# One attention-and-convolution kernel: fillers freed of the accumulator bank, a gate step in four operations, and more score sets in 29-row form

## The chip, the cores and the metric

The kernel runs on one core of a Trainium2 chip. The core has a matrix engine (PE, with its weight loads listed apart as PEld), a vector engine (DVE), a scalar engine (ACT), a general engine (POOL, which here mostly issues DMAs) and a queue engine (SP) that issues DMAs. Each engine works through its own instructions in the order in which they were written; semaphores hold an instruction until what it needs has been done. The metric is the time of one execution on the device in microseconds (us), the median over repeated runs.

## The reference

A row of the input gets an attention result `a` and a state-space convolution result `b`, mixed by a gate of one number for each row:

```python
S, D, H, Dh, N = 2048, 448, 16, 28, 256
q = (x @ wq).reshape(B, S, H, Dh).transpose(0, 2, 1, 3)
k, v = x @ wk, x @ wv                         # one key and one value head for all 16 query heads
scores = einsum("bhqd,bkd->bhqk", q, k) * Dh ** -0.5
a = (softmax(scores) @ v).transpose(0, 2, 1, 3).reshape(B, S, H * Dh) @ wo

dt = exp(log_dt)[:, None]
P = exp((dt * (A_re + 1j * A_im))[:, :, None] * arange(S))
K = einsum("dn,dnl,dn->dl", C, P, dt * Bc).real   # one kernel of 2048 taps for each channel
b = causal_convolution(x, K) + x * Dskip

g = sigmoid((x * gate_w).sum(-1, keepdims=True))
out = g * a + (1 - g) * b
```

All inputs and the output are bf16.

## The kernel before

**Attention.** The 2048 queries by 16 heads against 2048 keys are cut into 1024 score tiles of 128 keys by 512 columns. Sixteen groups of 64 tiles follow one another; a group is 512 queries by four heads, and its tiles run over 16 key tiles and the four heads (`h = t % 4`). The tiles are taken in 410 *sets*, by turns of three tiles (even sets) and two (odd sets). For each set:

- PE writes the scores into PSUM (`psS`, five banks in rotation). There are two forms. The *full form* (`full`, L1380) multiplies 128 rows of `kT` by a masked copy of the queries, `qM`, in which the rows of all other heads are zero; the two or three matmuls of a set run one after the other. The *29-row form* (`row`, L1357) takes the 29 rows of the tile's head alone, at rows 32h of the array, so that the matmuls of a set, having different heads, lie in different row strips and run side by side. `qM` is filled by a DMA from `qT`, so that the first tiles of a group have to use the 29-row form in any case (`NEWQ = 15`). The last 24 tiles are cut otherwise and have lines of their own (L1368).
- ACT takes the exp of the whole set into a ring of 15 tiles in SBUF (`expT`, L1412). Each exp needs its scores and free places in the ring.
- PE multiplies four exp tiles with the values (*PV*, L1433) and adds them up in the accumulator bank `psB` (key `("b", 6)`) over the 16 key tiles. At the end of a group DVE copies the bank out (`norm`, L1157), and the softmax's denominators, normalisation and output projection (L1137) follow.

**Convolution.** Beside this, DVE builds tables of powers for 32 channels at a time (`tables`, L972 to L1008, in 14 rounds), PE turns them into convolution kernels (`kgen`, L1031), and these are written to a scratch tensor in DRAM and read back as Toeplitz tiles `T` by SP's DMAs. PE convolves with them (`conv`, L1098, and L1119 for the transposed result), and DVE adds the result to the output tiles. `conv` number c first writes half c % 2 of the buffer `cst`; the other use of its second half is to hold the zeros that the fillers below read.

**The gate.** `prep_gate` transposes 1 - g by a matmul (L749), copies it, and spreads it with four small f32 matmuls (L760) in one operation. A copy of the result, `omq`, scales the convolutions. The two PE operations are placed behind sets 30 and 35 (`GATE`).

**Fillers.** Two kinds of matmul add zeros or write into unused banks, to keep PE busy. `warm` (L1333, 43 of them) is an operation of its own behind some of the first 64 sets; it adds zeros to the accumulator bank and declares that it writes that bank, so a PV that comes later in the program is ordered behind it, and it behind the PV before. `filler` (L1339) is put in by the planner where it finds a gap on PE.

**Order.** A planner written in Python, `Prog.schedule`, fixes the order of each engine before the program is written out. Each operation has an estimated length, a priority `pr` (small is early), its dependences by keys that it reads and writes, and an array mode (`mode`: "q" for 29-row, "c" for PV and convolution, "h" for `kgen`, "f" for full). It takes, over all engines, the operation that can start first; among those that can start at the same time the smallest `pr`. Score sets have 0, PV 0.5, `kgen` 1.15, `conv` 1.6, `warm` 1.95, the gate 2. `pg.after[a] = b` keeps a behind b in the plan. A dependence between two operations of PE orders them and needs no semaphore. `psb` marks the operations of the accumulator bank: 1 for a PV in the midst of a group, 2 for its last one; `opened` is true while a group is being added up. `act` is the share of its time that an operation counts in the planner's measure of how busy PE was, which must be under 0.8 over 4 us for a planner's filler.

Of the kernel before, what the change touches and what calls it, by code (L numbers as in the profile page):

```python
# [12 lines left out]
P = 128  # L13
# [32 lines left out]
XDVE = ((1, 0), (1, 1), (1, 2))  # L46
WARM = 64
HELD = ((27, 3), (27, 9), (27, 15), (27, 21))
ROWS = 400
NEWQ = 15  # L50
LASTQ = 13
STORES = (338, 341, 366)
# [43 lines left out]
class Prog:  # L96
# [15 lines left out]
    LAZY = {1.15: 200.0, 1.55: 200.0, 1.58: 200.0, 1.6: 200.0}  # L112
    LATE = 1000.0
    FILL, FWIN, FLOW = 215.0, 4000.0, 0.8

    def __init__(self, nc, es):
        self.nc, self.es = nc, es
# [70 lines left out]
    def schedule(self):  # L188
        ops = self.ops
# [11 lines left out]
        ready = {e: [] for e in ENG}  # L201
# [22 lines left out]
        while done < n:  # L224
            best = None
            for e in ENG:
                T = free[e]
                for i in ready[e]:
                    o = ops[i]
                    r = max(rt[i], T)  # L230
                    if o.lock is not None:
                        L = min((x for x in locks if x[0] is None), key=lambda x: x[1], default=None)
                        if L is None:
                            continue
                        r = max(r, L[1] + (300.0 if o.pr >= 2 else 0.0))
                    for k in o.comm or ():
                        if k in comm:
                            r = max(r, ops[comm[k]].end)
                    if e == "pe":
                        j = (npe + o.ni - self.FIRST - 1) // self.BLOCK + 1  # L240
                        if j < len(block):
                            r = max(r, block[j])
                            if o.pr >= 1 and block[-1] > r:
                                left = self.FIRST + (len(block) - 2) * self.BLOCK - npe - o.ni
                                r = max(r, block[-1] - left / self.NEED)
                    if o.slot is not None and o.slot[0] == "T" and self.spaced[0] < r < self.spaced[1]:
                        r = max(r, lastT + self.GAP)
                    key = (r, o.pr, i)
                    if best is None or key < best[0]:
                        best = (key, e, i)  # L250
# [25 lines left out]
                mode = o.mode  # L276
            if e == "pe":
                past.append((r, r + o.ns * o.act))
                opened = o.psb == 1 if o.psb else opened
            if e == "pool" and o.slot is None:  # L280
                for d in reversed(order[e]):
                    if ops[d].slot is None:
# [148 lines left out]
class Kernel:  # L431
# [311 lines left out]
    def prep_gate(self):  # L743
        pg = self.pg
        X = ("gx",)
        px = self.grp()
        ogT = Sub(self.acc, 512)
        self.gate = []
        o = pg.op("pe", lambda e: e.matmul(px.v(0, 16, 0, [[1, 128]]), self.gt.v(0, P, 16, [[1, 16]]),  # L749
                                       self.identg.v(0, P, 0, [[1, P]]), start=True, stop=True, tile_position=(0, 0),  # L750
                                       skip_group_check=True), 400,
              rd=["og", ("kst", 0)], wr=[X], pr=2, lock=px)
        self.gate.append(o.i)
        pg.op("dve", lambda e: e.tensor_copy(ogT.v(0, 16, 0, [[1, 128]]), px.v(0, 16, 0, [[1, 128]])), 200,
              rd=[X], wr=[("acc", 1)], pr=2)

        def mm(e):
            for mu in range(2):
                for par in range(2):
                    r = e.matmul(px.v(0, P, 64 * mu, [[1, 64]]), self.sel.v(0, 16, 128 * (1 + (1 - mu) - par), [[1, P]]),  # L760
                                 ogT.v(0, 16, 64 * par, [[1, 64]]), start=(par == 0), stop=(par == 1), tile_position=(0, 0),
                                 skip_group_check=True)
            return r
        o = pg.op("pe", mm, 800, rd=[("acc", 1)] + [("sel", k) for k in range(3)], wr=[X, "onw"], pr=2)
        self.gate.append(o.i)
        pg.op("dve", lambda e: e.tensor_copy(self.omq.v(0, P, 0, [[1, 128]]), px.v(0, P, 0, [[1, 128]])), 200,
              rd=[X], wr=["omq"], pr=2, unlock=px)
# [543 lines left out]
    def main(self):  # L1311
# [32 lines left out]
        def qk(s):  # L1344
            ts = sets[s]
            bs = [bank[t] for t in ts]
            bk = [("b", b) for b in bs]

            def row(e):
                if ts[0] >= NLAST:  # L1350
                    for x in range(2):
                        for t, b in zip(ts, bs):
                            r = part(e, t, b, x, True)
                    return r
                for t, b in zip(ts, bs):
                    i, kt, h = dec(t)
                    r = e.matmul(self.psS.v(0, P, 512 * b, [[1, 512]]),  # L1357
                                 kT.v(32 * h, DH + 1, 128 * kt, [[1, 128]]),
                                 qT.v(32 * h, DH + 1, 512 * (i % 2), [[1, 512]]),
                                 start=True, stop=True, tile_position=(32 * h, 0), skip_group_check=True)  # L1360
                return r

            def part(e, t, b, x, row):
                half, kt, h = declast(t)
                kt += x
                o = self.psS.v(0, P, 512 * b + 256 * x, [[1, 256]])
                if row:
                    return e.matmul(o, kT.v(32 * h, DH + 1, 128 * kt, [[1, 128]]),  # L1368
                                    qT.v(32 * h, DH + 1, 512 + 256 * half, [[1, 256]]),
                                    start=True, stop=True, tile_position=(32 * h, 0), skip_group_check=True)  # L1370
                return e.matmul(o, kT.v(0, P, 128 * kt, [[1, 128]]),
                                self.qM.v(0, P, XQ + 512 * h + 256 * half, [[1, 256]]),
                                start=True, stop=True, tile_position=(0, 0), skip_group_check=True)

            def full(e, t, b):
                if t >= NLAST:
                    part(e, t, b, 0, False)
                    return part(e, t, b, 1, False)
                i, kt, h = dec(t)
                return e.matmul(self.psS.v(0, P, 512 * b, [[1, 512]]), kT.v(0, P, 128 * kt, [[1, 128]]),  # L1380
                                self.qM.v(0, P, (i % 2) * XQ + 512 * h, [[1, 512]]),
                                start=True, stop=True, tile_position=(0, 0), skip_group_check=True)
            if s < 6 or s >= 14 and (len(ts) == 3 or ts[0] % 64 < NEWQ or s >= ROWS):
                rd = set()
                for t in ts:
                    i, kt, h = dec(t)
                    rd |= {("q", i % 2), ("kT", (kt if t < NLAST else declast(t)[1]) // 4)}
                o = pg.op("pe", row, 220, rd=sorted(rd, key=str), wr=bk, pr=0, mode="q", ni=2 * len(ts))
                o.act = 0.25 * len(ts)
            else:  # L1390
                for t, b in zip(ts, bs):
                    i, kt, h = dec(t)
                    kt = kt if t < NLAST else declast(t)[1]
                    o = pg.op("pe", lambda e, t=t, b=b: full(e, t, b), 220, rd=[("qM", i % 2), ("kT", kt // 4)],
                              wr=[("b", b)], pr=0, mode="f", ni=2)
            if s in GATE:
                pg.after[self.gate[GATE.index(s)]] = o.i
            if s < WARM and ts[0] % 64 < 52 and (ts[0] < 64 or ts[0] % 64 > 14):
                f = pg.op("pe", warm, 215, rd=[("cst", 1), "id"], wr=[("b", 6)], pr=1.95)
                pg.after[f.i] = o.i  # L1400
            if s == len(sets) - 2:
                pg.after[o.i] = self.prevset
            self.prevset = o.i
            if s in STORES:
                self.hold.append(o.i)
            es = [ring[t] for t in ts]
            ew = [("e", x) for x in es]
            for t in ts:
                x = ring[t] if t <= RING else 0
                ew += ["Wk"] if x == RING - 1 else ["Wv", "Wvg", "Wm"] if x == RING - 2 else self.xk(2) if 9 <= x < 13 else self.xk(3) if 5 <= x < 9 else []  # L1410
            n = len(ts)
            o = pg.op("act", lambda e: e.activation(expT.v(0, P, 512 * es[0], spread(es, n)),  # L1412
                                                self.psS.v(0, P, 512 * bs[0], spread(bs, n)),
                                                AF.Exp, scale=SQ), 46 + 428 * n, rd=bk, wr=ew, pr=0)
            self.lastexp = o.i
# [118 lines left out]
```

## Time and profile before

| | |
|---|---|
| median of 3 runs | 501.09 us (500.85 to 501.88) |
| the profiled execution | 500.49 us |
| its span in the profile | 498.7 us |
| first exp starts, last exp ends (L1412) | 21.71 us, 492.41 us |
| score matmuls in full form (L1380) | 316, each 383 ns |
| score matmuls in 29-row form (L1357) | 684, each 385 ns |
| fillers L1333, L1339 into the accumulator bank | 43 and 146 |
| DVE, last table instruction (L1008) | 447.94 us |

The span begins at the first instruction and ends with the last. A row of a group has the line of the kernel, the engine and operation, what is written and read, shapes, the count, and behind the bar the busy time in us, the mean of one in ns, and the idle time of the engine just ahead of them with what ended it. A row of the timeline has the start in us, the time that the merged instructions cover in us, engine, line, operation, and in brackets the idle time before it and what ended that. Times of matmuls overlap: a matmul of 512 columns is shown with some 0.38 us, while the next one in a run starts 0.22 us after it.

The granted clock of PE over some stretches (each line: the stretch, its length, busy us and instructions of each engine, the clock, the share of the DMA engines, GB/s):

```profile
26.00:34.00 8.00, 7.68 (x42) 2.26 (x40) 8.00 (x14) 7.76 (x7) 0.59 (x1) 1.00 0.38 46
76.00:100.00 24.00, 23.51 (x294) 9.05 (x295) 23.90 (x40) 24.00 (x22) 8.59 (x17) 1.00 0.80 230
447.00:480.00 33.00, 31.93 (x779) 17.74 (x777) 8.86 (x17) 31.98 (x29) 5.23 (x10) 1.00 0.80 238
```

The engines stand in the order PE, PEld, DVE, ACT, POOL.

### The profile page before, as it was taken

The page shows a single profiled execution, that of the slowest core. Times are in us where ns is not written, and L with a number is a line of the kernel's source. Part 1 is how long each engine was busy: PE and PEld are TensorE (multiplying, and loading weights), DVE is VectorE, ACT ScalarE, POOL GpSimd, SP SyncE. Part 2 cuts the span into 40 slices and gives each one's busy share as a digit, 9 for nine tenths or more (in the row PEclk, how much of TensorE's full clock was granted, in tenths as well). Part 3 has the DMA queues.
Part 4 walks back from the last instruction along what each step waited for, and adds up shares of the span by engine and source line. Part 5 has one row for each costly group of instructions (what it writes and reads, how often), then busy time and mean ns, then how long its engine had stood idle before and what let it go on. Part 6 is the DMA issues. An engine that isn't in the chain of part 4 may idle for free.

```text
span 498.7 us, 17357 instructions
## 1 busy us (share of the span) xinstructions
PE 478.2 (96%) x7643; PEld 217.7 (44%) x7643; DVE 456.0 (91%) x868; ACT 484.6 (97%) x436; POOL 197.5 (40%) x362
## 2 busy tenths in 40 slices
PE   8899999999999999999999999999999999999997
PEld 6432242453434435453452543545334354445543
DVE  6999999999999999999999999989999999992225
ACT  6999989999999999999999999999999999999995
POOL 8411034342242466276265456552733342521110
PEclk9999999999999999999999999999999999999999
DMA  8945008719248783945729595594690849657842
GB/s 252 268 57 113 1 16 229 213 34 315 77 118 265 204 217 87 308 108 165 242 36 268 155 288 138 141 220 112 171 265 19 231 129 340 213 164 215 257 131 70
DMA packets 91767, 85.44 MB, mean 171 GB/s; under 512 B 24970, under 2 KB 86716, under 8 KB 91692
## 3 DMA queue, kind: packets, MB, share of 16 engines
q1 hardware_dynamic: 80794, 72.49, 49.8%
q0 software_dynamic: 10624, 11.70, 10.5%
q8 instruction: 60, 0.98, 0.8%
q10 hardware_dynamic: 274, 0.14, 0.1%
q14 instruction: 15, 0.12, 0.1%
HBM read 76.36 MB, written 5.23 MB: 164 GB/s over the span
## 4 chain that ended last, share of the span: by engine, by line
ACT 77%; PE 15%; DMA 2%; SPq 0%; issue 0%
ACT expT L1412 77%; PE psS L1380 2%; PE psS L1357 2%; PE psB L1433 2%; DMA T<-KP_scratch 2%; PE psX L1098 1%; PE psS L1098 1%; PE psS L1031 1%; PE psB L1333 1%; PE psS L1368 1%; PE psS L1242 0%; PE psB L1427 0%; SPq L166 0%; PE psX L1031 0%; PE psX L1119 0%; PE psB L1339 0%
## 5 line engine op out<-in xcount | busy, mean ns | idle before, releaser
L1412 ACT ACTIVATE expT<-psS 128x1536 bf16<-128x1536 f32 (+1 forms) x410 | 464.8, 1363 | 3.5 <-PE psS L1357 1.4
L972 DVE TENSOR_TENSOR tab<-tab,mbf 128x512 bf16<-128x512 bf16 (+4 forms) x140 | 139.2, 996 | 0.0
L1357 PE MATMUL psS<-qT,kT 29*128 29x512 bf16 x684 | 95.7, 385 | 10.5 <-ACT expT L1412 6.4
L1433 PE MATMUL psB<-expT,vaug 128*32 128x512 bf16 x1000 | 99.7, 390 | 0.2 <-DVE acc L1157 0.2
L1380 PE MATMUL psS<-qM,kT 128*128 128x512 bf16 x316 | 95.1, 383 | 0.8
L166 POOL DMA_DIRECT2D KP_scratch<-kstg x104 | 58.1, 565 | 75.5 <-DVE kstg L1043 74.0
L987 DVE TENSOR_TENSOR tab<-tab 128x256 bf16<-128x256 bf16 (+4 forms) x140 | 77.0, 571 | 0.0
L1433 PEld LDWEIGHTS psB<-expT,vaug 128*32 128x32 bf16 x1000 | 25.6, 93 | 72.9 <-issue 69.9
L1357 PEld LDWEIGHTS psS<-qT,kT 29*128 29x128 bf16 x684 | 23.7, 91 | 62.9 <-ACT expT L1412 51.9
L166 POOL DMA_DIRECT2D U<-in_A_x_dram x60 | 39.9, 669 | 25.0 <-DMA U<-in_A_x_dram 10.3
L166 POOL DMA_DIRECT2D qM<-qT x64 | 32.5, 516 | 39.4 <-DVE qT L889 29.3
L1339 PE MATMUL psB<-ident,one 128*128 128x512 bf16 x146 | 47.2, 384 | 0.0
L1098 PEld LDWEIGHTS psS<-T,U 128*26 128x26 bf16 (+3 forms) x1792 | 35.7, 138 | 14.9 <-issue 10.2
L166 POOL DMA_DIRECT2D rdenB<-R_scratch x60 | 31.0, 523 | 28.0 <-DMA R_scratch<-denT 27.9
L1098 PE MATMUL psS<-T,U 128*26 128x128 bf16 (+3 forms) x1792 | 41.0, 226 | 1.1 <-DMA T<-KP_scratch 1.1
L1098 PE MATMUL psX<-T,U 128*26 128x128 bf16 (+3 forms) x1600 | 38.9, 227 | 0.7 <-issue 0.7
L1098 PEld LDWEIGHTS psX<-T,U 128*26 128x26 bf16 (+3 forms) x1600 | 32.6, 139 | 11.9 <-issue 9.5
L166 POOL DMA_DIRECT2D denT<-acc x15 | 10.8, 717 | 56.4 <-DVE acc L1157 47.7
L1001 DVE TENSOR_TENSOR tab<-tab,tmp 128x1984 bf16<-128x1984 bf16 x28 | 32.5, 1177 | 0.0
L1380 PEld LDWEIGHTS psS<-qM,kT 128*128 128x128 bf16 x316 | 19.5, 97 | 24.8 <-ACT expT L1412 15.3
L995 DVE TENSOR_TENSOR tmp<-tmp,mq 128x64 bf16<-128x64 bf16 (+4 forms) x70 | 25.3, 361 | 0.3
L918 DVE TENSOR_TENSOR msq<-T 128x512 f32<-128x512 f32 (+1 forms) x40 | 24.6, 616 | 0.0
(191 smaller groups left out, 511.9 us busy)
## 6 DMA issues: line engine op xcount, KB each, us to landing
T<-KP_scratch SPq DMA_DIRECT2D x212, 272.0 KB, 5.6
rdenB<-R_scratch POOLq DMA_DIRECT2D x60, 64.0 KB, 2.5
U<-KP_scratch SPq DMA_DIRECT2D x12, 272.0 KB, 4.9
U<-in_A_x_dram SPq DMA_DIRECT2D x20, 112.0 KB, 4.6
qM<-qT POOLq DMA_DIRECT2D x64, 32.0 KB, 3.9
tab<-in_A_x_dram SPq DMA_DIRECT2D x4, 448.0 KB, 5.2
KP_scratch<-kstg POOLq DMA_DIRECT2D x104, 16.0 KB, 1.7
xT<-XS_scratch POOLq DMA_DIRECT2D x3, 448.0 KB, 4.3
```

The lines of the kernel that those rows point to most:

```text
L166: return [e.dma_start(o, i, **kw) for o, i in pairs]
L918: pg.op("dve", lambda e: e.tensor_tensor(m2(msq), z2, z2, ALU.mult), el(2 * n), rd=[kr, ki] + first, wr=["msq"], pr=pr)
L972: mul = lambda e, o, a, b: e.tensor_tensor(o, a, b, ALU.mult)
L987: vo(lambda e, dv=dv, tv=tv, k=k: e.tensor_tensor(dv, dv, tv, ALU.add if k else ALU.subtract), n, [kt[k], kd[k]], [kd[k]], 1.92 if lv else ...
L995: vo(lambda e, w=w, lv=lv: e.tensor_tensor(rho.v(0, P, (32 - 2 * w) * 2, [[64, 32], [2, w], [1, 2]]), rho.v(0, P, (32 - w) * 2, [[64, 32], ...
L1001: vo(lambda e, k=k: e.tensor_tensor(tab.v(0, P, FM + k * FP + 2, [[64, 32], [2, 31], [1, 2]]), tab.v(0, P, lm + k * PL + 62, [[64, 32], [- ...
L1098: r = e.matmul(ps.v(32 * j, 32 - m0, 128 * k, [[1, 128]]), self.U.v(0, P, (4 * gi + j) % UA // UC * UW + (2 * m0 + par) * UC + (4 * gi + j ...
L1339: return e.matmul(t.v(0, P, off, [[1, 512]]), self.one.v(0, P, 2, [[0, P]]), self.ident.v(0, P, 0, [[0, 4], [1, P]]), start=b != 6, stop=b ...
L1357: r = e.matmul(self.psS.v(0, P, 512 * b, [[1, 512]]), kT.v(32 * h, DH + 1, 128 * kt, [[1, 128]]), qT.v(32 * h, DH + 1, 512 * (i % 2), [[1, ...
L1380: return e.matmul(self.psS.v(0, P, 512 * b, [[1, 512]]), kT.v(0, P, 128 * kt, [[1, 128]]), self.qM.v(0, P, (i % 2) * XQ + 512 * h, [[1, 51 ...
L1412: o = pg.op("act", lambda e: e.activation(expT.v(0, P, 512 * es[0], spread(es, n)), self.psS.v(0, P, 512 * bs[0], spread(bs, n)), AF.Exp, ...
L1433: r = e.matmul(self.psB.v(32 * h, 32, 0, [[1, 512]]), vaug.v(0, P, 32 * kt, [[1, 32]]), expT.v(0, P, 512 * ring[t], [[1, 512]]), start=(kt ...
```

## The change

Four things, in the order of the diff below.

`ROWS` goes from 400 to 320, and the condition on the form of a set is written anew: every three-tile set takes the 29-row form (before, sets 6, 8, 10 and 12 had the full form), and so do the two-tile sets from 320 on (before, from 400 on). 74 of the 316 matmuls in full form change.

`warm` no longer declares a write of the accumulator bank. It gets `psb = 3` instead: the planner places such an operation only while a group is open, and where an operation of priority 0 or less on PE is due to become ready in the first 175 ns of the filler (its 215 ns less `NEAR` = 40), it counts the filler as ready only behind that operation. A filler does not change `opened`.

The four small matmuls of the gate become four operations of 200 ns each in the plan, in place of one of 800 ns. The first is kept behind set 35; the others follow by their dependence.

```diff
-ROWS = 400
+ROWS = 320
...
     FILL, FWIN, FLOW = 215.0, 4000.0, 0.8
+    NEAR = 40.0
...
+                    if o.psb == 3:
+                        if not opened:
+                            continue
+                        for x in ready["pe"]:
+                            if ops[x].pr <= 0.0 and r < rt[x] < r + o.ns - self.NEAR:
+                                r = max(rt[x], T) + ops[x].ns
...
-                opened = o.psb == 1 if o.psb else opened
+                opened = o.psb == 1 if o.psb in (1, 2) else opened
...
-        def mm(e):
-            for mu in range(2):
-                for par in range(2):
-                    r = e.matmul(px.v(0, P, 64 * mu, [[1, 64]]), self.sel.v(0, 16, 128 * (1 + (1 - mu) - par), [[1, P]]),
-                                 ogT.v(0, 16, 64 * par, [[1, 64]]), start=(par == 0), stop=(par == 1), tile_position=(0, 0),
-                                 skip_group_check=True)
-            return r
-        o = pg.op("pe", mm, 800, rd=[("acc", 1)] + [("sel", k) for k in range(3)], wr=[X, "onw"], pr=2)
+        for mu in range(2):
+            for par in range(2):
+                o = pg.op("pe", lambda e, mu=mu, par=par: e.matmul(
+                    px.v(0, P, 64 * mu, [[1, 64]]), self.sel.v(0, 16, 128 * (1 + (1 - mu) - par), [[1, P]]),
+                    ogT.v(0, 16, 64 * par, [[1, 64]]), start=(par == 0), stop=(par == 1), tile_position=(0, 0),
+                    skip_group_check=True), 200, rd=[("acc", 1)] + [("sel", k) for k in range(3)], wr=[X, "onw"], pr=2)
+                if mu + par == 0:
+                    o1 = o
+        o = o1
         self.gate.append(o.i)
...
-            if s < 6 or s >= 14 and (len(ts) == 3 or ts[0] % 64 < NEWQ or s >= ROWS):
+            if s < 6 or len(ts) == 3 or s >= 14 and (ts[0] % 64 < NEWQ or s >= ROWS):
...
-                f = pg.op("pe", warm, 215, rd=[("cst", 1), "id"], wr=[("b", 6)], pr=1.95)
+                f = pg.op("pe", warm, 215, rd=[("cst", 1), "id"], pr=1.95)
+                f.psb = 3
                 pg.after[f.i] = o.i
```

## The prediction

> **What bounds the kernel now.** I read the page first (busy shares, then the chain of waits), then the groups by shape on the scalar engine, then the timeline of PE and ACT at each place where an exp starts late.
>
> ```profile
> PE 478.2 (96%) x7643; PEld 217.7 (44%) x7643; DVE 456.0 (91%) x868; ACT 484.6 (97%) x436; POOL 197.5 (40%) x362
> ...
> ACT 77%; PE 15%; DMA 2%; SPq 0%; issue 0%
> ...
> L1412 ACT ACTIVATE expT<-psS 128x1536 bf16<-128x1536 f32 x205 | 322.8, 1575 | 2.8 <-PE psS L1357 1.4 <-PE psB L1433 1.1 <-PE psS L1380 0.2
> L1412 ACT ACTIVATE expT<-psS 128x1024 bf16<-128x1024 f32 x204 | 235.6, 1155 | 0.7 <-PE psS L1380 0.6
> ```
>
> The 410 exps of L1412 set the span: 77% of the chain is theirs. They run one into the next, so a group's mean (1575 ns) is longer than the step to the next start. Start to start the medians are 1.33 us after a three-tile set and 0.90 after a two-tile set. What a change of PE's order can win is therefore only the time by which starts fall behind these steps. Summed from the start times, after set 0, that is 8.8 us (counting only steps over 40 ns late), in some forty places; the columns above show 3.5 us of it as idle. The change touches four kinds of place.
>
> ```profile
> 33.16 0.81 PE L1380 MATMUL psS<-qM,kT 128*128 128x512 bf16 x3
> 33.80 0.38 PE L1333 MATMUL psB<-ident,cst 128*128 128x512 bf16 x1
> 34.01 7.11 ACT L1412 ACTIVATE expT<-psS 128x1536 bf16<-128x1536 f32 x6 [0.16 <-PE psS L1380]
> ...
> 40.26 0.39 PE L1357 MATMUL psS<-qT,kT 29*128 29x512 bf16 x3 [0.24 <-ACT expT L1412]
> 40.58 0.39 PE L1333 MATMUL psB<-ident,cst 128*128 128x512 bf16 x1
> ...
> 64.85 0.77 PE L760 MATMUL psS<-acc,onT 16*128 16x64 f32 x5
> ...
> 66.20 6.88 ACT L1412 ACTIVATE expT<-psS 128x1536 bf16<-128x1536 f32 x6 [0.23 <-PE psS L1357]
> ...
> 68.36 0.40 PE L1433 MATMUL psB<-expT,vaug 128*32 128x512 bf16 x4
> ...
> 72.78 0.60 PE L1333 MATMUL psB<-ident,cst 128*128 128x512 bf16 x2
> ...
> 73.74 0.40 PE L1433 MATMUL psB<-expT,vaug 128*32 128x512 bf16 x4
> ...
> 74.19 1.45 ACT L1412 ACTIVATE expT<-psS 128x1536 bf16<-128x1536 f32 x1 [1.11 <-PE psB L1433]
> ```
>
> In the first group set 8 (three full matmuls, 33.16) ends where its exp begins: the exp waits for PE. In the second, the gate's eight records (five and, further on, three, 64.85 to 65.8) stand ahead of the last matmul of set 36, whose exp starts at 66.20. In the third, no PV runs between 68.36 and 73.74; a PV outranks the kernel-generation matmuls that run in that hole (priority 0.5 against 1.15), so a dependence held it, and it comes just after two fillers of L1333, which write its bank. The exp of set 42 needed the ring slots that this PV frees.
>
> **The sum, part by part.**
>
> *Three-tile sets 6, 8, 10, 12.* The full form takes 0.64 us of PE (33.16 to the filler at 33.80), the 29-row form 0.32 (40.26 to 40.58). The exps after sets 5, 7, 9, 11 start 0.13, 0.27, 0.13 and 0.11 late, 0.64 in all, each released by the full set. With 0.32 less each is on time, unless a filler stands ahead. Bounds 0.2 (the 0.27 stays, and fillers eat half of the rest) to 0.64; I take 0.55, as the filler now also steps aside for a set due within 175 ns. The row of 40.26 has a change of array form on both sides.
>
> [...]
>
> *The gate.* Set 36 started 0.53 us late. Each of the four operations is two records 0.11 us apart, some 0.23 us. If only the first stands ahead of set 36, nothing is lost; with two or three, 0.1 to 0.3. I take 0.45 (0.2 to 0.53). The remaining three go where nothing else is ready; their reader (the copy to omq) is needed first by the convolution at 86.7 us, so they have 20 us of cover.
>
> *Fillers off the bank.* Set 42 started 1.27 us late. With the dependence gone the PV goes ahead of generation and fillers. Bounds 0 (the hole has another cause) to 1.3; I take 1.1. The other side of it: the 43 fillers, lowest in priority, pile up, and the second convolution overwrites the zeros they read, so it must be placed behind all of them; the last ran at 98.2 us. PE is 98% busy there (23.5 of 24 us), so that convolution may start some us later; DVE has its tables to build meanwhile. I cost this at nothing; if DVE stood behind it, it would be a late table, not a late exp.
>
> *Two-tile sets from 320.*
>
> ```profile
> 448.44 0.60 PE L1380 MATMUL psS<-qM,kT 128*128 128x512 bf16 x2
> 448.98 0.51 PE L1098 MATMUL psX<-T,U 128*30 128x128 bf16 x20
> ...
> 462.28 0.39 PE L1357 MATMUL psS<-qT,kT 29*128 29x512 bf16 x2
> 462.59 0.40 PE L1433 MATMUL psB<-expT,vaug 128*32 128x512 bf16 x4
> ...
> 469.69 0.44 PE L1098 MATMUL psX<-T,U 128*30 128x128 bf16 x15 [0.69 <-issue]
> ...
> 470.71 1.02 ACT L1412 ACTIVATE expT<-psS 128x1024 bf16<-128x1024 f32 x1 [0.63 <-PE psS L1380]
> ...
> 448.56 0.42 DVE L1128 TENSOR_TENSOR O<-O,psS 128x256 bf16<-128x256 bf16 x1
> ```
>
> A full pair takes 0.54 us, a 29-row pair 0.31. Of the odd sets from 321 to 399, 31 change (the nine others are in the form already): 31 x 0.22 = 6.8 us of PE. Most of it is hidden, since ACT sets the pace until 447 us; 26 planner fillers between 389 and 480 show that PE had room. From 447 on the chain runs on PE. From set 321 on exps start 2.7 us late in all, the largest 0.77 and 0.29 around the stall at 469 and 0.36 at set 396. The stall ends in a wait the profile names only "issue" and will fall elsewhere; a pair behind it is 0.22 sooner. I take 0.8, bounds -1 (the new order draws a worse stall, like the 1.1 us below) to 2.0.
>
> *Does the early gain arrive?* The first three terms, 2.1 us, bring ACT forward, but not DVE, which is busy throughout and ends its tables at 448.6 us. The convolutions behind it then have 2.1 us less. PE between 448.6 and 492 gets back 12 pairs x 0.22 = 2.6 us, three fillers (1.0) and 0.9 of issue stalls: enough, without much to spare. So cost nothing; uncovered it would be the first rival.
>
> Sum: 0.55 + 0.45 + 1.1 + 0.8 = 2.9 us. The profiled execution took 500.49 (span 498.7), so 497.6; the median of the runs stands 0.60 above it, which makes **498.2**. The ends of the four terms add up to 0.6 us lost and 4.5 us gained; the forecast's own range is 497.0 to 500.0.
>
> **Rivals.**
>
> *The late crowd.* The early 2.1 us are handed back between 447 and 492, because the freed PE time before is filled with more fillers (a 29-row pair counts half in the planner's busy share) and the last tables come no sooner. For: DVE at 448.6, and PE chain after. Against: the budget above. Then some 0.4 us remain: 500.7.
>
> *Convolutions ahead of their data.* This ends slower. PE runs in order, so a convolution whose Toeplitz tile has not landed holds the next score set.
>
> ```profile
> 327.50 0.40 PE L1098 MATMUL psS<-T,U 128*32 128x128 bf16 x12 [1.12 <-DMA T<-KP_scratch]
> ```
>
> PE waited 1.12 us for the tile at 327.50, which cost set 266 1.08 us; so much was lost once in 56 loads. With ACT 2 us ahead of DVE the order is drawn anew, and loads that depend on DVE's tables come later against the exps. Four new ones take more than the whole gain and the 0.2% on top; five give 501.09 - 2.9 + 5.4 = 503.6. For: that stall itself. Against: the planner places each convolution after its own estimate of the landing, and only one in 56 fails now.
>
> *The clock.* The granted clock reads 1.00 from 6.45 us on. Three fillers at 24.2 and 25.8 us lie ahead of the first PV (27.36) and can't be placed there any more. If the clock halved for 4 us in 26 to 34, where PE is busy 7.68 of 8 us, some 3 us of stalls would eat the gain: 501.2. Against: in 12 to 14 us PE was busy 0.87 of 2, with transposes and the first of a group of matmuls, at clock 1.00, and 461.8 to 468.4 has six sets in a row in 29-row form at 1.00.
>
> [...]
>
> That the change does not do what it says (the PV hole stays) makes 499.3, inside the forecast's range.
>
> **How the numbers follow.** Forecast 0.68, the late crowd 0.14, convolutions ahead of data 0.12, the clock 0.06. A measurement here can tell about 0.2% (1.0 us) from no change. Faster by more: 0.68. Within: crowd 0.14, most of the clock 0.04, few stalls 0.01: 0.19. Slower: 0.11 + 0.02 = 0.13. The range runs from 496.9 (late exps nearly all gone, about 0.05 below it) to 501.7, which takes in the crowd and the clock and leaves out some 0.14.
>
> **What would show it.** Right: the exp of set 42 starts without a wait on a PV, no PV gap over 3 us near 70; set 36 follows 35 by 0.90; sets 6 to 12 on L1357; L1380 falls from 316 to 242 matmuls and L1357 rises from 684 to 758; the last exp ends near 489.5 instead of 492.4. Wrong: new idle before L1412 between 76 and 447 that a DMA or a convolution ends; last exp near 492; a clock under 1.00 before the end; many more of L1339's fillers after 389.

## The result, and the profile after

The changed kernel took 498.20 us (median of 5 runs, 496.54 to 498.56) beside 501.01 for the kernel before in the same runs (500.31 to 501.88): a ratio of 0.9933, 95% interval 0.9912 to 0.9955. Its profiled execution took 496.92 us, span 495.2, against 500.49 and 498.7. That pair differs by 3.57 us, the medians by 2.8. Below, the trace accounts for the 3.57. Medians here and below are over all runs, while a ratio leaves out a run that is over 1.5% above the fastest of its kernel.

The line numbers of the changed kernel are six to nine higher: the exps are L1421, the 29-row form L1365, the full form L1388, PV L1442, the fillers L1341 and L1347, the gate's matmuls L766. First the page of the changed kernel (busy times, shares of the chain, groups), then its exps by shape:

```profile
PE 474.8 (96%) x7647; PEld 217.4 (44%) x7647; DVE 455.7 (92%) x868; ACT 483.4 (98%) x436; POOL 196.6 (40%) x362
...
ACT 90%; PE 3%; DMA 1%; SPq 1%; DVE 0%; issue 0%
...
L1365 PE MATMUL psS<-qT,kT 29*128 29x512 bf16 x758 | 109.5, 385 | 10.7 <-ACT expT L1421 6.4
...
L1388 PE MATMUL psS<-qM,kT 128*128 128x512 bf16 x242 | 73.1, 384 | 0.7 <-ACT expT L1421 0.4
```

```profile
L1421 ACT ACTIVATE expT<-psS 128x1536 bf16<-128x1536 f32 x205 | 321.8, 1570 | 0.4 <-PE psS L1365 0.2
L1421 ACT ACTIVATE expT<-psS 128x1024 bf16<-128x1024 f32 x204 | 234.6, 1150 | 0.0
```

The chain is now 90% exps, where it was 77%, and the idle time ahead of the exps is 0.4 us in all, from 3.5. The counts of the two forms moved by the 74 matmuls of the diff. PE is busy 3.4 us less.

Where the time came from is seen in the start times of the exps. The table sums by how much each step from one start to the next exceeds 1.33 us (after a three-tile set) or 0.90 (after a two-tile set), steps over 40 ns late alone; it is worked out from the start times in the traces, in us. The step from set 0 to set 1, 3.93 us in both, is left out.

| sets | before | after | difference |
|---|---|---|---|
| 1 to 5 | 0.31 | 0.31 | 0 |
| 6 to 13 | 0.65 | 0 | 0.65 |
| set 36 (gate) | 0.53 | 0.19 | 0.34 |
| set 42 (fillers) | 1.27 | 0 | 1.27 |
| others from 14 to 100 | 0.71 | 0.61 | 0.10 |
| 100 to 200 | 0.79 | 1.11 | -0.32 |
| 200 to 321 | 1.87 | 1.16 | 0.71 |
| 321 to 409 | 2.67 | 1.05 | 1.62 |
| sum | 8.80 | 4.43 | 4.37 |

The last exp ends at 488.35 us instead of 492.41, 4.06 earlier (the first started 0.13 later, and the last one took 0.74 us in place of 0.59). What follows the last exp grew from 6.34 to 6.83 us. So 4.06 - 0.49 = 3.57.

Two places of the changed kernel's timeline, PE around sets 36 and 42:

```profile
64.47 0.32 PE L766 MATMUL psS<-acc,onT 16*128 16x64 f32 x1
64.62 0.39 PE L1365 MATMUL psS<-qT,kT 29*128 29x512 bf16 x2
64.63 0.49 PE L766 MATMUL psS<-acc,onT 16*128 16x64 f32 x3
64.96 0.38 PE L1365 MATMUL psS<-qT,kT 29*128 29x512 bf16 x1
65.27 0.40 PE L1442 MATMUL psB<-expT,vaug 128*32 128x512 bf16 x4
65.60 0.43 PE L766 MATMUL psS<-acc,onT 16*128 16x64 f32 x2
...
69.72 0.40 PE L1442 MATMUL psB<-expT,vaug 128*32 128x512 bf16 x4
70.05 0.42 PE L1039 MATMUL psX<-tab 128*64 128x128 bf16 x8
70.40 0.60 PE L1388 MATMUL psS<-qM,kT 128*128 128x512 bf16 x2
70.94 0.40 PE L1442 MATMUL psB<-expT,vaug 128*32 128x512 bf16 x4
71.27 0.43 PE L1039 MATMUL psX<-tab 128*64 128x128 bf16 x8
```

Four records of the gate, two operations, still stand ahead of the last matmul of set 36 (64.96); the other two operations went behind it. The PV hole of 5.4 us between 68.36 and 73.74 is gone: PV runs at 69.72 and 70.94, between the steps of kernel generation.

And the end, in the timeline of the changed kernel (PE and DVE):

```profile
489.08 0.55 PE L1210 MATMUL psS<-msq,acc 128*128 128x4 f32 x4
489.10 0.62 DVE L1298 TENSOR_TENSOR O<-O,psX 128x448 bf16<-128x448 bf16 x1
...
489.63 0.61 DVE L1298 TENSOR_TENSOR O<-O,psS 128x448 bf16<-128x448 bf16 x1
...
490.17 0.20 DVE L1236 RECIPROCAL T<-psS 128x8 f32<-128x8 f32 x1
```

The reciprocal (L1236) needs the last denominators, which PE has written by 489.63 (L1210), but DVE takes a second addition to an output tile (L1298) first: some 0.5 us. Before, the chain after the last exp ran over PE's matmuls and the last scaling on ACT, with no addition in it.

### The profile page after: what moved, and what is told of

It reads as the page before. It is cut to its first block, busy times and chain, and to the rows that moved or that the text cites. A ratio compares the mean times of both kernels' runs of the same rounds, so it can differ in the third digit from the quotient of the medians.

```text
span 495.2 us, 17358 instructions
## 1 busy us (share of the span) xinstructions
PE 474.8 (96%) x7647; PEld 217.4 (44%) x7647; DVE 455.7 (92%) x868; ACT 483.4 (98%) x436; POOL 196.6 (40%) x362
## 4 chain that ended last, share of the span: by engine, by line
ACT 90%; PE 3%; DMA 1%; SPq 1%; DVE 0%; issue 0%
ACT expT L1421 90%; DMA U<-KP_scratch 1%; PE psS L1365 1%; PE psS L1106 1%; SPq L167 1%; PE psB L1442 0%; PE psB L1347 0%; PE psX L1039 0%; DVE O L1298 0%; PE psS L1278 0%; PE psS L1225 0%; ACT O L1301 0%; PE psX L894 0%; PE psS L1217 0%; PE psX L1278 0%
## 5 line engine op out<-in xcount | busy, mean ns | idle before, releaser
L1421 ACT ACTIVATE expT<-psS 128x1536 bf16<-128x1536 f32 (+1 forms) x410 | 463.7, 1359 | 0.4 <-PE psS L1365 0.2
L1365 PE MATMUL psS<-qT,kT 29*128 29x512 bf16 x758 | 109.5, 385 | 10.7 <-ACT expT L1421 6.4
L1442 PE MATMUL psB<-expT,vaug 128*32 128x512 bf16 x1000 | 99.9, 390 | 0.0
L1388 PE MATMUL psS<-qM,kT 128*128 128x512 bf16 x242 | 73.1, 384 | 0.7 <-ACT expT L1421 0.4
L1365 PEld LDWEIGHTS psS<-qT,kT 29*128 29x128 bf16 x758 | 27.2, 91 | 68.4 <-ACT expT L1421 55.3
L1442 PEld LDWEIGHTS psB<-expT,vaug 128*32 128x32 bf16 x1000 | 25.6, 93 | 68.6 <-issue 66.7
L1347 PE MATMUL psB<-ident,one 128*128 128x512 bf16 x147 | 48.4, 384 | 0.0
L1106 PE MATMUL psS<-T,U 128*26 128x128 bf16 (+3 forms) x1792 | 43.1, 227 | 0.0
L1388 PEld LDWEIGHTS psS<-qM,kT 128*128 128x128 bf16 x242 | 14.6, 97 | 18.7 <-ACT expT L1421 12.0
```

The lines of the kernel that those rows point to most:

```text
L1106: r = e.matmul(ps.v(32 * j, 32 - m0, 128 * k, [[1, 128]]), self.U.v(0, P, (4 * gi + j) % UA // UC * UW + (2 * m0 + par) * UC + (4 * gi + j ...
L1347: return e.matmul(t.v(0, P, off, [[1, 512]]), self.one.v(0, P, 2, [[0, P]]), self.ident.v(0, P, 0, [[0, 4], [1, P]]), start=b != 6, stop=b ...
L1365: r = e.matmul(self.psS.v(0, P, 512 * b, [[1, 512]]), kT.v(32 * h, DH + 1, 128 * kt, [[1, 128]]), qT.v(32 * h, DH + 1, 512 * (i % 2), [[1, ...
L1442: r = e.matmul(self.psB.v(32 * h, 32, 0, [[1, 512]]), vaug.v(0, P, 32 * kt, [[1, 32]]), expT.v(0, P, 512 * ring[t], [[1, 512]]), start=(kt ...
```

## The experiments

Each kernel was timed beside the kernel before on the same chip; ratios are to that. The three groups of kernels ran on three chips. The kernel before had medians of 500.35, 500.34 and 500.69 us in them, so ratios compare better than times.

**One part undone at a time.** Four kernels, each the changed one with one part as it was:

```diff
noR
-ROWS = 320
+ROWS = 400
noW
-                f = pg.op("pe", warm, 215, rd=[("cst", 1), "id"], pr=1.95)
-                f.psb = 3
+                f = pg.op("pe", warm, 215, rd=[("cst", 1), "id"], wr=[("b", 6)], pr=1.95)
noG   (the gate as one operation of four matmuls)
+        o = pg.op("pe", mm, 800, rd=[("acc", 1)] + [("sel", k) for k in range(3)], wr=[X, "onw"], pr=2)
noT
-            if s < 6 or len(ts) == 3 or s >= 14 and (ts[0] % 64 < NEWQ or s >= ROWS):
+            if s < 6 or s >= 14 and (len(ts) == 3 or ts[0] % 64 < NEWQ or s >= ROWS):
```

> The changed kernel with two-tile sets in full form again up to set 399 (ROWS = 400). Sum by places: the early places stay mended (sets 6 to 12, 36 and 42 on time, 2.3 us), only the lateness from set 321 on comes back (2.7 us in the kernel before, 1.1 in the changed one): about 1.6 us slower than the changed kernel, 499.8. Late crowd: DVE ends its tables near 448.5 us whatever the early exps do, so without the freed 6.8 us of PE the early gain is handed back behind 447 us: early places mended, but the last exp near 491 to 492 and the time 500.5 to 501. Redrawn order: the difference lies in transfers or fetches that fall badly, with no tie to the stage behind 389 us.

> The changed kernel with the 43 warm fillers writing the accumulator bank again. Sum by places: the PV hole near 70 us comes back and the exp of set 42 starts about 1.3 us late; 499.5. Rival: the hole came from the gate's single operation or from kernel generation, and stays away: 498.2. A third way: PE makes up for it later, so that the place shows 1.3 us but the end no more than 0.5.

> The changed kernel with the gate's four matmuls in one operation again. Sum by places: set 36 starts 0.53 us late in place of 0.19; 498.5, inside what can be told apart. Rival: the gate was what starved the PVs behind it, and set 42 is late again too: 499.5 or more.

> The changed kernel with sets 6, 8, 10 and 12 in full form again. Sum by places: exps of sets 6, 8, 10 and 12 late by 0.1 to 0.3 us each, 0.5 to 0.65 together; 498.8. Rival: with fillers that step aside the full form would be on time too, except by the 0.3 us that it is longer where PE starts at the release of the banks: 0.3 or less; 498.4.

| kernel | median us | ratio (95%) | late: 6 to 13 | set 36 | set 42 | 100 to 321 | 321 to 409 |
|---|---|---|---|---|---|---|---|
| changed | 498.20 | 0.9933 (0.9912 to 0.9955) | 0 | 0.19 | 0 | 2.27 | 1.05 |
| noR | 496.88 | 0.9938 (0.9920 to 0.9956) | 0.26 | 0.19 | 0 | 2.38 | 1.22 |
| noW | 500.19 | 1.0000 (0.9983 to 1.0016) | 0 | 0.09 | 1.77 | 3.69 | 2.14 |
| noG | 505.41 | 1.0092 (1.0067 to 1.0117) | 0.16 | 0.64 | 0 | 2.39 | 2.59 |
| noT | 498.49 | 0.9970 (0.9953 to 0.9988) | 0.68 | 0.20 | 0 | 3.75 | 0.76 |

Each of the three early parts brings its own stall back in its own place: 0.68 us at sets 6 to 13 in noT, 0.64 at set 36 in noG, 1.77 at set 42 in noW. There the exp of set 42 again waits for a PV that comes just behind a filler (PE and ACT of noW; the filler is L1341, PV L1441):

```profile
67.66 0.40 PE L1441 MATMUL psB<-expT,vaug 128*32 128x512 bf16 x4
...
72.97 0.38 PE L1341 MATMUL psB<-ident,cst 128*128 128x512 bf16 x1
73.28 0.40 PE L1441 MATMUL psB<-expT,vaug 128*32 128x512 bf16 x4
...
73.74 6.88 ACT L1420 ACTIVATE expT<-psS 128x1536 bf16<-128x1536 f32 x6 [1.50 <-PE psB L1441]
```

The form of the two-tile sets brings nothing back: without it the ratio is the same, and the late stalls are 1.22 us instead of 1.05. But the totals do not follow from the places. (In noT, 1.5 us of the 3.75 stands in a stretch at half clock, 376.08 to 379.49 us, of which more below; the profile of noG has such a stretch too, at 27.25 us.) Without the fillers' part nothing is left of the gain; without the gate's part the kernel is nearly 5 us slower than before. The kernels differ elsewhere too, since the planner draws the whole order anew from any change.

**Why noG is slower.** In noG the convolutions went on until 497.6 us; in the changed kernel they end at 485.1. PE's timeline in noG:

```profile
454.90 1.02 PE L1105 MATMUL psX<-T,U 128*32 128x128 bf16 x56
...
458.60 0.45 PE L1126 MATMUL psX<-ident,cst 128*64 128x64 bf16 x16
...
459.84 0.66 PE L1038 MATMUL psX<-tab 128*64 128x128 bf16 x16
```

The last kernel generation (L1038) starts at 459.84, only when convolution 24 or 25 has given back its PSUM bank by its transposition (L1126): both had taken a bank ahead of it. DVE's tables end at 451.24, so they are not what it waited for. Its result is written to DRAM and read back for the last convolutions, which come late by as much. The next kernel keeps the gate as one operation and adds one line to the list of convolutions that the planner holds back, so that convolution 25 waits too:

```diff
-HOLDC = (((24, 8), 7),)
+HOLDC = (((24, 8), 7), ((25, 0), 4))
```

> The changed kernel with the gate in one operation again, as noG, and one more line: convolution 25 may start only behind the first operation of the second half of the last kernel generation (round 13). In the trace of noG two convolutions hold both pooled PSUM banks when the last tables are done at 451.2 us, and generation starts at 459.8 in place of 450. If that is where the 8 us went, this kernel's last convolution ends near 485 to 486 and its time is that of the changed kernel plus the gate's 0.4 us, 498 to 499. If the gate's own operation did it, the time stays near 505.

PE's timeline in that kernel:

```profile
450.88 0.43 PE L1038 MATMUL psX<-tab 128*64 128x128 bf16 x8
```

Generation starts 9 us sooner, the last convolution ends at 486.44, and the time is 497.49 us, ratio 0.9944 (0.9926 to 0.9963), with set 36 still 0.64 late. So noG's loss was the bank order that came with it, not the gate's own operation. What the gate's part is worth by itself is less than these runs tell apart, and the changed kernel with the added line alone was not run.

**What the two-tile form saves in an order that stays.** In noR the planner knew of the full form and drew its order for it. The next kernel keeps the changed kernel's order to the instruction, and only at the end gives the 31 odd sets from 321 to 399 two full matmuls. Beside it the changed kernel itself was timed again ("again").

```diff
(in outline)
             self.pg.schedule()
+            for o, f, d in self.swap:     # the 31 sets; f: full(t, b) for each tile
+                o.fn = f                  # and a wait for d, the DMA that fills qM
```

> The changed kernel with its plan as it is, instruction for instruction in the same order on every engine; only the 31 two-tile sets from 321 to 399 that the change put in 29-row form are carried out in full form (two full matmuls). So 6.8 us more of PE work behind 389 us, and nothing redrawn. If PE time there is worth what the prediction took: exps from set 321 on fall behind by 0.8 us more, 499 us. Rival (the runs so far point to it: with the sets planned in full form the time was 496.9): ACT sets the pace and PE has that much room, so the last exp ends within 0.3 us of the changed kernel's, and the last convolution some 2 to 4 us later; the time as the changed kernel's in the same job.

> The changed kernel once more, beside the others of this job, to see how its times group. If a stretch of 3.4 us at half clock, which the profiles of two other kernels showed, comes and goes between executions, runs with a mean clock of 1.000 lie near 496.7 and those with 0.997 near 498.3; if the spread has another cause, time and clock are unrelated.

same_order_full took 500.51 us, ratio 1.0005 (0.9982 to 1.0027); the changed kernel 498.16, 0.9954 (0.9932 to 0.9976). In the fixed order the form is worth 2.35 us: exps from set 321 on were 5.14 us late against 1.45. The added wait does not seem to be the reason: its trace shows no matmul that waits for the DMA that fills `qM`. With an order drawn for the full form (noR) no worth can be told. The order is packed to the estimated lengths; 6.8 us of PE put back into it without a new order show in the time, 6.8 us that the planner knows of do not.

**The fillers' part alone, and the clock.** The profiled execution of "again" took 501.55 us, 4.6 more than that of the same program before. The windows of that trace, with PE's busy time and the granted clock in the column ahead of the DMA share:

```profile
23.77:27.18 3.41, 2.17 (x23) 1.06 (x22) 3.41 (x8) 3.41 (x5) 1.16 (x2) 1.00 0.92 205
27.18:30.59 3.41, 3.39 (x16) 0.72 (x16) 3.41 (x5) 2.52 (x3) 0.00 (x0) 0.50 0.56 76
30.59:34.01 3.42, 3.42 (x14) 0.62 (x10) 2.48 (x4) 2.28 (x2) 0.00 (x0) 0.50 0.30 15
34.01:37.42 3.41, 3.08 (x13) 0.82 (x11) 1.82 (x6) 2.31 (x2) 0.71 (x1) 0.50 0.25 12
37.42:40.83 3.41, 3.41 (x23) 1.03 (x23) 3.19 (x12) 2.95 (x4) 0.00 (x0) 1.00 0.87 166
```

At 27.18 us the clock halves for three stretches of 3.41 us. ACT is busy 2.5, 2.3 and 2.3 of 3.41 us in them instead of nearly all the time. Sets 1 to 13 are 4.32 us late, against 0.31 in the first trace of the same program. In the window ahead PE was busy 2.17 of 3.41 us: this is the gap that three early fillers, which now may not run before the first PV, have left. It is in the first trace too (the timeline of the changed kernel). That trace holds no record of the clock, and its mean of 1.000 is no reading (the same may hold for single runs given with 1.000 below); but its exps up to set 13 were only 0.31 us late, so a stretch like the one above is not in it:

```profile
25.54 0.57 PE L809 MATMUL psX<-ident,T 112*128 112x112 bf16 x8 [0.51 <-DVE tab L820]
26.85 0.39 PE L1365 MATMUL psS<-qT,kT 29*128 29x512 bf16 x2 [0.74 <-ACT expT L1421]
```

Two kernels put this to the test: the kernel before with the fillers' part alone, and the changed kernel with three matmuls of zeros written into the gap behind the transposes, once the order was made.

```diff
fillers_alone   (on the kernel before)
+    NEAR = 40.0
...
+                    if o.psb == 3:
...
-                f = pg.op("pe", warm, 215, rd=[("cst", 1), "id"], wr=[("b", 6)], pr=1.95)
+                f = pg.op("pe", warm, 215, rd=[("cst", 1), "id"], pr=1.95)
+                f.psb = 3
heat_gap   (on the changed kernel)
             self.pg.schedule()
...
+            o.fn = lambda e: (g(e), [e.matmul(self.psB.v(0, P, 0, [[1, 512]]), z.v(0, P, 2, [[0, P]]),
+                                              self.ident.v(0, P, 0, [[0, 4], [1, P]]), start=True, stop=True,
+                                              tile_position=(0, 0), skip_group_check=True) for _ in range(3)])[0]
```

> The kernel before with the fillers freed of the bank and nothing else of the change. Sum by places: set 42 on time (1.3 us), sets 8 to 12 a little better as fillers step aside, set 36 still 0.5 late: 1.3 to 1.6 us under the kernel before. Rival: the fillers are nearly all of it, since without them the change gained nothing: 2.5 to 3 us under. Third: the order drawn anew in the last stage takes it back or adds to it, by several us either way.

> The changed kernel in its own order, with three matmuls of zeros more, put behind the last transposes at 26.1 us, where PE waits 0.74 us for the exp of set 1; they write the accumulator bank before its first group opens. If the half-clock stretch comes from this gap, which the fillers can't fill any more, hardly any run has a mean clock under 0.998 and the median goes to 496.7; if it comes from later gaps too, as many as before, and the median stays near 498.

The fillers' part alone took 501.62 us, ratio 1.0012 (0.9994 to 1.0031): no gain, though set 42 was on time in it. Its mean granted clock was 0.997 or less in all 12 runs (one stretch of 3.41 us at half clock makes 0.997 of 495 us). The profiled run shows two, at 27.38 and 293.62 us; its exps were 3.19 us late between sets 200 and 321 and 3.78 from 321 on. With zeros in the gap the window looks like this (heat_gap):

```profile
23.77:27.18 3.41, 2.82 (x28) 1.35 (x28) 3.41 (x8) 3.41 (x5) 0.79 (x1) 1.00 0.85 179
27.18:30.59 3.41, 3.40 (x24) 0.95 (x20) 3.41 (x4) 3.35 (x4) 0.00 (x0) 1.00 0.31 19
```

heat_gap took 497.38 us, 0.9954 (0.9932 to 0.9976), the same ratio as "again". Its runs had a mean clock of 1.000 in 6 of 9, against 6 of 12: too few to tell. So the same zeros were tried where every run had been disturbed:

```diff
fillers_alone_heat: fillers_alone with the three matmuls of heat_gap
```

> The kernel before with the fillers alone freed (fillers_alone, all 12 of whose runs had a mean clock of 0.997 or less) and the three matmuls of zeros behind the last transposes at 26 us. If the gap of PE there lets the clock fall, most runs gain one half-clock stretch of 3.4 us of clock (mean clock up by 0.0034), the profile has none at 27 us, exps of sets 4 and 6 are no longer 0.5 to 0.9 late, and the time falls by 1 to 1.5 us to about 500. If not, clocks and times stay as in fillers_alone, 501.6. The order drawn anew behind 200 us stays as it was, so that it does not come down to 498.

It took 499.89 us, 0.9986 (0.9966 to 1.0006), and 5 of 12 runs had the clock at 1.000 (one at 0.999), where it was none of 12. In its profile the clock did not fall at 27 us, and sets 4 and 6 were 0.15 and 0.11 us late instead of 0.93 and 0.49; the other fall, in a stretch that the zeros do not touch, stayed (292.13). So in this kernel the gap can cost the clock, and filling it helped. Its five undisturbed runs lie at 497.87 to 499.94 us, eleven of the kernel before beside them at 499.01 to 500.53.

Why did the gap cost the clock in one execution and not in another? In every trace that shows changes of the clock before the end, they lie whole multiples of 3.41 us apart: in "again" the fall at 27.18 and the rise at 37.42 us by three (10.24), in fillers_alone the falls at 27.38 and 293.62 us by 78 (266.24). So I take it that they stand on a grid, and count it from the first record of the clock at 1.00, which lay anywhere from 3.77 to 6.90 us (6.45 in the kernel before). Two stretches so counted, the first from same_order_full, the second from noR:

```profile
23.56:26.97 3.41, 2.15 (x24) 1.06 (x21) 3.41 (x8) 3.41 (x5) 0.94 (x2) 1.00 0.94 201
23.05:26.47 3.42, 2.45 (x25) 1.06 (x22) 3.42 (x8) 3.42 (x6) 1.28 (x3) 1.00 0.92 201
```

In four kernels (again, noG, same_order_full, fillers_alone) one stretch of the grid held the whole gap, with PE busy for 2.15 to 2.17 us, and the clock fell behind it in all four. In noR, noT, gate_one_held and all_29_row the grid lay otherwise, the stretch had 2.24 to 2.50 us, and the clock stayed. In the five profiles with fillers or zeros in the gap (before, noW and the three with zeros) it had 2.80 or more, and the clock stayed.

That the change makes falls more frequent is not shown: in the group of "again" 6 of its 12 runs had a mean clock of 0.997 or less, and 13 of the 32 of the kernel before.

The clock explains much of the spread of one kernel. Of "again", six runs at 1.000 took 496.2 to 498.1 us, three at 0.997 498.2 to 499.2, two at 0.993 499.0 and 499.2, one at 0.990 501.6: by the medians 0.9 to 1.6 us for each stretch. The kernel before has such runs too: 16 of those 32 at 1.000 (498.7 to 500.9), 13 at 0.997 or less (500.3 to 503.2).

**The tail.** heat_gap with the addition of the last tile but one held behind the last reciprocal on DVE:

```diff
             pg.after[o2.i] = rc.i
+            pg.after[self.add1] = rc.i
...
```

> The changed kernel with the three matmuls of zeros in the gap, and with the second output addition of the last query block kept behind the last reciprocal on DVE (in the changed kernel the reciprocal waited for two additions, 0.55 us each, after the matmul before it had ended). The end behind the last exp shrinks from 6.8 to 6.3 us, what the kernel before had; runs without a half-clock stretch near 496.4, the median 496.5 to 497.5, under the changed kernel by 0.5 to 1.5. Rival: the last store waits for something else, and the end stays 6.8.

DVE's timeline in it:

```profile
490.91 0.62 DVE L1305 TENSOR_TENSOR O<-O,psX 128x448 bf16<-128x448 bf16 x1
491.49 0.21 DVE L1242 RECIPROCAL T<-psS 128x8 f32<-128x8 f32 x1
491.61 0.57 DVE L1305 TENSOR_TENSOR O<-O,psS 128x448 bf16<-128x448 bf16 x1
```

One addition now comes behind the reciprocal, and from the last exp to the end it is 6.41 us, not 6.83 (6.82 in heat_gap). The whole took 497.15 us, 0.9932 (0.9911 to 0.9953); its three runs at a clock of 0.999 or 1.000 were 496.45 to 496.59. It is the lowest ratio of all, but its interval overlaps that of the changed kernel. The gain of 0.42 us shows in the trace alone.

**All sets in 29-row form.** If 29-row sets are never worse, all could have the form from set 14 on:

```diff
-ROWS = 320
+ROWS = 14
```

> The changed kernel with every set in 29-row form (ROWS = 14): the 242 matmuls left in full form go. If PE time is worth little where ACT sets the pace, and the full form serves to keep PE busy for its clock, then no gain: runs at clock 1.000 within 0.5 us of the changed kernel's 496.9, and more runs with half-clock stretches, median 498 to 500. If the score sets' PE time is what delays exps, the small lateness between 100 and 409 (3.3 us in the changed kernel) falls by half and the time goes to 495 to 496.

It took 500.63 us, 0.9994 (0.9965 to 1.0022). The profiled execution was undisturbed until its end and its exps were 5.50 us late, 4.43 in the changed kernel. But 10 of 12 runs had a mean clock of 0.997 or less, down to 0.986 (504.0 us) and, once, 0.976 (508.1); the two at 0.999 and 1.000 took 496.8 and 497.9. So at full clock the form cost little, and with the full matmuls gone the clock fell more often than in "again" (6 of 12). Whether the form or the order drawn anew does that is not shown, and no trace shows where.

## Why the prediction came true, and where it did not

*Total and direction.* 498.2 us was forecast and measured. Part of that agreement is luck. The profiled execution gained 3.57 us where the sum had 2.9, and the median stood 1.28 us above it where 0.60 was taken over from the kernel before; the two misses cancel. One term has its gain from elsewhere, and effects that are not in the sum (redrawn orders, the clock, the tail) came in besides.

*Three-tile sets, 0.55 us.* Right: 0.65 went, at the places named, and 0.68 came back with the form in noT. That fillers step aside was not needed for it: in noW they do not, and nothing is late there.

*The gate, 0.45 us.* Right in kind, a little large: 0.34, because two of the four operations stay ahead of set 36's last matmul, the case that the bounds named. Set 36 followed set 35 by 1.09 us, not by the 0.90 named as a sign. In the whole time nothing of it can be told (gate_one_held).

*Fillers off the bank, 1.1 us.* Right in place, 1.27 by the trace, and noW shows that the dependence was the cause. The other side was put at nothing, and there the step left something out. The fillers piling up behind were harmless as said; the gap that the three early ones left at 24 to 27 us was harmless in some executions only. In fillers_alone no gain was left: the clock fell in every run, and the new order had 7.0 us of late exps from set 200 on (4.6 in the kernel before), 1.1 of them at a stretch at half clock.

*Two-tile sets from 320, 0.8 us.* This step failed. The stalls there did fall, by 1.62 us, but nearly as much without the form (1.22 us late in noR, 1.05 with it, from 2.67). It was treated as time given back to a fixed order, in which it would be worth 2.35 us; the order is drawn for what it is told, and between noR and the changed kernel no difference is measured. So the late stalls shrank with the new order that the other parts bring about. Which of them did it stays open: with any one undone the order differs.

*The early gain arrives.* Right: DVE's last table instruction ends at 449.25 us (448.64 before), yet the last exp ends 4.06 us sooner and the last convolution at 485.1, where it was 489.5. The late crowd did not come, with 31 planner's fillers between 389 and 480 us for 26. The given reason is not the full one: noR has the last exp at 488.66 without the 2.6 us of PE that the two-tile sets were to give back.

*Convolutions ahead of their data.* Did not occur in the changed kernel; the stall of set 266 even went with the redrawn order, which leaves 0.71 us less in all for sets 200 to 321. That a redrawn order can cost more than the change brings was the right fear with the wrong mechanism: noG lost some 7 us in one, by the order of PSUM banks and not by loads that came late by themselves.

*The clock, chance 0.06.* The rival was named at its place, 26 to 34 us, and the reasons against it did not hold. In 6 of 12 runs of "again" the mean clock was under 1.000, and the profiled one shows it fall there, behind a stretch with matmuls for 2.17 us of 3.41. That the clock stayed at 12 to 14 us proved nothing for 24 to 27 us: in every profile with a record of the clock, one stretch of the grid begun between 10 and 14 us had only 1.96 to 2.48 us with matmuls, and no fall came behind it. The price, 3 us, was twice that of one stretch (1.5 us) and less than that of three (4.3). Since runs of the kernel before are disturbed nearly as often, the difference of the medians does not show it. (The clock of the kernel before does not read 1.00 to the end, as the prediction has it, but to 497.97 us, and 0.50 behind that; nothing in the sum hangs on it.)

*Not in the sum:* the tail's 0.49 us, lost because DVE takes the last reciprocal after two additions.

## What to carry to other kernels

When a planner draws the whole order from estimates, the parts of a change don't add: look up each part's stall in its own place in the trace, and judge the whole only by the whole, with one kernel that keeps the order fixed where a part's worth is disputed. Time taken off an engine that the planner already balances may be worth nothing that can be measured, as here with the two-tile sets, unless a wait ends on it. When a filler is moved, ask what keeps the matrix engine busy in the gap that it leaves (here 1.2 us without a matmul at 25 to 27 us went with a fall of the clock in four of eight profiles), and read the granted clock over several executions, since one profile may miss the fall.

## What the hardware showed that was not expected

The granted clock fell to half for 3.41 us or a whole multiple (10.24 us in "again") behind stretches in which PE was far from idle. Leaving out the last 5 us of each span, the traces show ten falls, in eight kernels, and in the 3.41 us just ahead of them PE was shown busy for 2.15 to 2.90 us, 63 to 85% of it. An example from heat_and_tail:

```profile
112.70:116.11 3.41, 2.28 (x30) 0.90 (x28) 3.41 (x9) 3.41 (x4) 1.03 (x2) 1.00 1.04 338
116.11:119.53 3.42, 3.42 (x13) 0.66 (x9) 3.42 (x8) 3.19 (x3) 1.78 (x4) 0.50 0.96 283
```

No threshold follows from this: in "again" a stretch with 2.47 us shown busy, from 13.53 on, drew no fall behind it, nor did one with 1.96 us from 12.24 on in fillers_alone_heat, while noT fell at 376.08 after 2.77. The clock fell in one execution of a program and not in another (in "again" 6 of 12 runs had a mean of 0.997 or less); for the gap at 24 to 27 us the place of the 3.41 us stretches against the program, which differs from run to run, told the two apart in all eight profiles that have the gap and a record of the clock (PE busy for 2.15 to 2.17 us in the stretch that held the gap where the clock fell behind it, 2.24 to 2.50 where it stayed).
